# Longer contiguous pieces per partition in the weight loads of a one-token decode block

## The chip, the cores and the metric

The kernel runs on one core of a Trainium2 chip. The metric is the device time of one execution in microseconds (us): the median of three runs of the kernel before is 101.41 us, and the three lie between 101.40 and 101.51 us. A profile of one further execution was taken; it ran 101.79 us, of which 100.5 us lie between its first and its last instruction (the span). The other 1.3 us are start and end of the launch.

## The reference

One token (a row `x` of 1024 numbers) goes through an attention block with a key and value cache and through a two-layer perceptron; both read the same normalised row and both results are added to `x`. Everything is bf16.

```python
xn = _layernorm(x)                                   # 1 x 1024
# attention over the last W = 4096 cached positions, 32 query heads on 4 key/value heads
q = (xn @ wq)                                        # 1024 x 4096: 32 heads of 128
k = repeat(k_cache[:, :, Sk - W:, :], 8); v = repeat(v_cache[:, :, Sk - W:, :], 8)
p = softmax(q . k * 128 ** -0.5)
a = (p . v).reshape(1, 4096) @ wo                    # 4096 x 1024
# perceptron on a second layer norm
h = gelu(_layernorm(xn) @ w1 + b1)                   # 1024 x 3584
m = h @ w2 + b2                                      # 3584 x 1024
out = x + a + m
```

With a single row there is hardly any arithmetic per byte. The weights and the cache that are read come to 39.86 MB: wq 8.4 MB, w1 7.3 MB, keys 4.2 MB, values 4.2 MB, w2 7.3 MB, wo 8.4 MB.

## The kernel before, in words

**Layout of the weights.** Each weight matrix is spread over the 128 partitions so that one partition holds consecutive rows of the matrix: 8 rows of wq, 8 rows of w1, 28 rows of w2, 32 rows of wo. What one partition needs therefore lies in one contiguous piece of the memory. A list of numbers (`WQ_CHUNKS`, `W1_CHUNKS`, `W2_CHUNKS`, `WO_CHUNKS`, lines 22 to 25) says in how many loads a matrix comes and how many rows per partition each load brings. `load_rows` (line 142) issues one DMA per number. A chunk of 2 rows of wq is a piece of 16 KB for each of the 128 partitions; a chunk of 2 rows of w1 is 14 KB; 9 rows of w2 are 18 KB; 8 rows of wo are 16 KB. Each load has a semaphore of its own, and the matrix engine waits for it before the first matmul that reads the chunk.

**The order of the loads.** All big loads are issued by SyncE (SP) on one queue: four of wq, four of w1, two of keys, two of values (line 204). SP then waits until the matmuls on w1 are done (`sp.wait_ge(PE.sem, C["h"])`, line 316), because w2 is put over w1 and wo is put over wq in the on-chip memory, and issues four of w2 and six of wo. The two biases and the row `x` come on ScalarE's queue (lines 152 to 154).

**The order of the matmuls.** TensorE (PE) runs one program in order: the layer norm's sums; the bias b1 as the start of the accumulators (line 271, after a wait for its load); wq chunk by chunk (line 279, 8 matmuls of 512 columns a row, 64 in all); w1 chunk by chunk (line 294, 7 matmuls a row, 56 in all); the transposes of the keys (line 370) and of h (line 335); the scores (line 396); the first chunk of w2 (line 437, 4 matmuls of 256 columns a row, each on its own quarter of the array's columns); the softmax's total (line 450); the values (line 460, 64 matmuls); the second chunk of w2; the transpose of the attention's result (line 477); the other chunks of w2; and wo chunk by chunk (line 437 again, 128 matmuls in all). All of w2 and wo adds up in one accumulator, which ScalarE copies out (line 492) and SP stores (line 494). VectorE (DVE) and ScalarE (ACT) do the softmax between the scores and the values (lines 402 to 424).

**Matmuls without a use.** After chunk `j` of wo, PE runs the matmuls that `KEEP_BUSY[j]` lists (line 488). They read data that is there already and write to a bank of the accumulator memory that nobody reads any more; the list has one entry for each chunk of wo, six after the second chunk and four after the third.

Of the kernel before, what the change touches and what calls it, by code (L numbers as in the profile page):

```python
# [18 lines left out]
FC = F // 128  # L19
KC = D // 128  # L20
NQ = HQ * DH
WQ_CHUNKS = [2, 2, 2, 2]
W1_CHUNKS = [2, 2, 2, 2]
W2_CHUNKS = [9, 9, 8, 2]
WO_CHUNKS = [8, 8, 8, 6, 1, 1]
KEEP_BUSY = [[], [512] * 6, [512] * 4, [], [], []]
NPAIR = HKV // 2
PB = 2 * NBLK
OUTSIDE = -1e30
# [15 lines left out]
def bass_parallel_sum__sliding_block_cached__mixer_channel_mlp__decode_kernel(  # L45
# [20 lines left out]
    def sems(name, n):  # L66
        return [nc.alloc_semaphore(f"{name}{i}") for i in range(n)]

    s_xrow, s_b1, s_b2, s_out = (nc.alloc_semaphore(n) for n in ("s_xrow", "s_b1", "s_b2", "s_out"))
    s_wq = sems("s_wq", len(WQ_CHUNKS))  # L70
    s_w1 = sems("s_w1", len(W1_CHUNKS))
    s_k = sems("s_k", NPAIR)
    s_v = sems("s_v", NPAIR)
    s_wo = sems("s_wo", len(WO_CHUNKS))
    s_w2 = sems("s_w2", len(W2_CHUNKS))

# [65 lines left out]
    def load_rows(dst, src, chunks, width, semaphores):  # L142
        c0 = 0
        for j, n in enumerate(chunks):
            sp.dma_start(  # L145
                dst[:, c0 * width:(c0 + n) * width].rearrange("p (c n) -> p c n", c=n),
                src[:, c0:c0 + n, :],
            ).then_inc(semaphores[j], 16)
            c0 += n
# [49 lines left out]

    load_rows(WA, wq_p, WQ_CHUNKS, NQ, s_wq)  # L200
    load_rows(W1, w1_p, W1_CHUNKS, F, s_w1)
    for dst, cache, semaphores in ((KT, A_k_cache, s_k), (V, A_v_cache, s_v)):
# [71 lines left out]
    k = 0  # L274
    for j, n in enumerate(WQ_CHUNKS):
        pe.wait_ge(s_wq[j], 16)
# [12 lines left out]
    k = 0  # L289
    for j, n in enumerate(W1_CHUNKS):  # L290
        pe.wait_ge(s_w1[j], 16)
# [24 lines left out]
    sp.wait_ge(PE.sem, C["h"])  # L316
    load_rows(W2, w2_p, W2_CHUNKS, D, s_w2)
    load_rows(WA, wo_p, WO_CHUNKS, D, s_wo)

# [112 lines left out]
    def out_rows_mms(weights, vec, chunks, semaphores, j, stop_at=None):  # L432
        c0 = sum(chunks[:j])
        pe.wait_ge(semaphores[j], 16)
        for c in range(c0, c0 + chunks[j]):
            for a in range(4):
                ins = pe.matmul(acc(a), lhsT=vec[:, c:c + 32],  # L437
                                rhs=weights[:, c * D + a * 256: c * D + (a + 1) * 256],
                                start=False, stop=(c == stop_at))
        return ins  # L440
# [6 lines left out]
    pe.wait_ge(DVE.sem, C["d_GT"])  # L447
    out_rows_mms(W2, GT, W2_CHUNKS, s_w2, 0)
    pe.wait_ge(DVE.sem, C["sump"])
# [21 lines left out]
    with nc.allow_low_precision(reason="one of the two terms is not zero"):  # L471
        C["on"] = DVE.mark(dve.tensor_reduce(
            out=ON[:, :], in_=ONM[:, :].rearrange("p (g d) -> p d g", g=NPAIR), axis=AX.X, op=ALU.add))
    out_rows_mms(W2, GT, W2_CHUNKS, s_w2, 1)
    pe.wait_ge(DVE.sem, C["on"])
# [5 lines left out]
    C["OT"] = DVE.mark(dve.tensor_copy(OT[:, 0:32], PS[:, 5 * 512:5 * 512 + 32]))  # L481
    for j in range(2, len(W2_CHUNKS)):
        out_rows_mms(W2, GT, W2_CHUNKS, s_w2, j)
    pe.wait_ge(DVE.sem, C["OT"])
    for j in range(len(WO_CHUNKS)):
        last = out_rows_mms(WA, OT, WO_CHUNKS, s_wo, j, stop_at=31)
        for n in KEEP_BUSY[j]:
            pe.matmul(PS[0:32, 0:n], lhsT=OT[:, 0:32], rhs=WA[:, 0:n])
# [37 lines left out]
```

## Time and profile before

| What | Value |
|---|---|
| median of three runs | 101.41 us |
| the profiled execution | 101.79 us |
| its span | 100.5 us |
| PE busy | 70.3 us of the span |
| DVE, ACT busy | 25.4 and 12.8 us |
| bytes read, mean rate | 39.86 MB, 397 GB/s |
| packets on SP's load queue | 3176 |
| granted clock of PE, mean | 0.881 |

How to read it: PE, DVE, ACT, POOL and SP are the engines; "PEld" is PE's loading of the stationary operand, which overlaps its matmuls. The DMA share is the mean busy share of the 16 DMA engines that one core has; a packet is one contiguous piece that one of them moves. The granted clock is the share of full speed that TensorE was given. A chain of waits is followed back from the last instruction: at each step to what released it. Times inside the profile are counted from the start of the span.

### The profile page before, as it was taken

Reading aid. Unit: us, or ns where it says so; the run is one execution under the profiler, and the core shown is the slowest. Engines: PE = TensorE matmul, PEld = TensorE weight load, DVE = VectorE, ACT = ScalarE, POOL = GpSimd, SP = SyncE. Lnnn points to the kernel's source line nnn. Section 1 sums busy time; section 2 is a strip of 40 time slices with the busy share of each in tenths; the row PEclk is TensorE's granted clock in tenths of the full one; section 3 lists DMA queues with packets and bytes.
Section 4 is the critical chain, followed back from the end, with each engine's and each line's share of the span. In section 5 each row is a group of like instructions: output and inputs, shape, how many; then the busy total and the mean of one; then the engine's idle time right before and its main releaser. Section 6 shows DMA issues by size and latency. Waiting matters only on the chain.

```text
span 100.5 us, 1676 instructions
## 1 busy us (share of the span) xinstructions
PE 70.3 (70%) x762; PEld 41.3 (41%) x762; DVE 25.4 (25%) x48; ACT 12.8 (13%) x15; POOL 5.6 (6%) x22
## 2 busy tenths in 40 slices
PE   1309999999995738664999891652099999081961
PEld 1204224344332212224999591250078887041440
DVE  0574000000100000035859608474900030000000
ACT  2203300000000000031717600015000000000001
POOL 6870000000000000000000000000000000000000
PEclk9999999999999999999999985555557999999655
DMA  3999999999999999999999999999999999999920
GB/s 99 385 440 430 417 424 417 443 441 416 428 422 423 428 422 436 424 430 443 424 450 417 417 452 403 418 462 395 425 398 463 417 424 430 417 430 412 391 83 1
DMA packets 3188, 39.96 MB, mean 397 GB/s; under 512 B 359, under 2 KB 363, under 8 KB 750
## 3 DMA queue, kind: packets, MB, share of 16 engines
q1 hardware_dynamic: 3176, 39.85, 93.9%
q8 instruction: 6, 0.10, 0.4%
q10 hardware_dynamic: 6, 0.01, 0.0%
HBM read 39.86 MB, written 0.00 MB: 396 GB/s over the span
## 4 chain that ended last, share of the span: by engine, by line
DMA 82%; SPq 9%; PE 5%; issue 1%; ACT 0%
DMA WA<-in_A_wo_dram 45%; DMA W<-in_B_w_dram 37%; SPq L145 9%; PE PS L294 3%; PE PS L437 2%; ACT ORow L492 0%; PE PS L303 0%
## 5 line engine op out<-in xcount | busy, mean ns | idle before, releaser
L279 PE MATMUL PS<-WA,XNZ 128*8 128x512 bf16 x64 | 15.9, 415 | 0.0
L294 PE MATMUL PS<-W,YTb 128*1 128x512 bf16 x56 | 12.7, 379 | 4.3 <-DMA W<-in_B_w_dram 4.3
L279 PEld LDWEIGHTS PS<-WA,XNZ 128*8 128x8 bf16 x64 | 5.9, 93 | 10.4 <-issue 3.5
L294 PEld LDWEIGHTS PS<-W,YTb 128*1 128x1 bf16 x56 | 4.4, 83 | 12.7 <-DMA W<-in_B_w_dram 5.8
L437 PE MATMUL PS<-WA,OT 128*32 128x256 bf16 x128 | 5.1, 309 | 6.1 <-DMA WA<-in_A_wo_dram 6.1
L370 PE MATMUL PS<-identb,KV 128*128 128x128 bf16 x128 | 7.5, 219 | 2.2 <-DVE ROW L309 2.2
L460 PE MATMUL PS<-KV,Pb 128*32 128x256 bf16 x64 | 8.8, 310 | 0.0
L370 PEld LDWEIGHTS PS<-identb,KV 128*128 128x128 bf16 x128 | 7.2, 98 | 2.3 <-ACT ROW L307 2.3
L460 PEld LDWEIGHTS PS<-KV,Pb 128*32 128x32 bf16 x64 | 7.0, 110 | 1.6
L437 PEld LDWEIGHTS PS<-WA,OT 128*32 128x32 bf16 x128 | 3.5, 107 | 8.1 <-DMA WA<-in_A_wo_dram 7.8
L377 DVE COPY KV<-PS 128x1024 bf16<-128x1024 bf16 x10 | 6.3, 683 | 1.5 <-PE PS L370 1.5
L309 DVE CAST ROW<-PS 1x2048 bf16<-1x2048 f32 x1 | 2.3, 2278 | 16.4 <-PE PS L294 16.4
L382 ACT ACTIVATE KV<-PS 128x1024 bf16<-128x1024 bf16 x6 | 5.8, 1018 | 2.8 <-PE PS L370 2.8
L307 ACT ACTIVATE ROW<-PS 1x1536 bf16<-1x1536 f32 x1 | 1.4, 1440 | 33.4 <-PE PS L294 33.4
L437 PE MATMUL PS<-W,GT 128*32 128x256 bf16 x112 | 4.9, 320 | 1.0 <-DMA W<-in_B_w_dram 1.0
L286 DVE CAST Q<-PS 8x512 bf16<-8x512 f32 x1 | 0.7, 679 | 17.4 <-PE PS L279 17.4
L437 PEld LDWEIGHTS PS<-W,GT 128*32 128x32 bf16 x112 | 3.5, 110 | 1.8 <-issue 1.5
L492 ACT ACTIVATE ORow<-PS 128x256 bf16<-128x256 f32 x1 | 0.4, 385 | 29.2 <-PE PS L437 29.2
L424 DVE TENSOR_REDUCE SUMP<-Pb 128x32 f32<-128x2048 bf16 x1 | 3.6, 3566 | 1.9 <-ACT Pb L422 1.9
L396 PEld LDWEIGHTS PS<-QT,KV 128*128 128x128 bf16 x128 | 3.3, 98 | 0.4 <-issue 0.4
L396 PE MATMUL PS<-QT,KV 128*128 128x16 bf16 x128 | 3.4, 171 | 0.0
L450 PE MATMUL PS<-onesf,SUMP 128*32 128x1 f32 x2 | 0.3, 202 | 4.4 <-DVE SUMP L424 4.4
(91 smaller groups left out, 44.8 us busy)
## 6 DMA issues: line engine op xcount, KB each, us to landing
WA<-in_A_wq_dram SPq DMA_DIRECT2D x4, 2048.0 KB, 14.0
W<-in_B_w_dram SPq DMA_DIRECT2D x4, 1792.0 KB, 30.6
WA<-in_A_wo_dram SPq DMA_DIRECT2D x3, 2048.0 KB, 41.1
W<-in_B_w_dram SPq DMA_DIRECT2D x2, 2304.0 KB, 24.5
KV<-in_A_k_cache_dram SPq DMA_DIRECT2D x2, 2048.0 KB, 43.2
KV<-in_A_v_cache_dram SPq DMA_DIRECT2D x2, 2048.0 KB, 47.4
W<-in_B_w_dram SPq DMA_DIRECT2D x1, 2048.0 KB, 31.5
WA<-in_A_wo_dram SPq DMA_DIRECT2D x1, 1536.0 KB, 45.6
```

The costliest lines, as they stand in the source:

```text
L145: sp.dma_start(dst[:, c0 * width:(c0 + n) * width].rearrange("p (c n) -> p c n", c=n), src[:, c0:c0 + n, :],).then_inc(semaphores[j], 16)
L279: last = pe.matmul(PS[0:8, 7 * 512:8 * 512], lhsT=XNZ[:, 15 * k + 7 - t:15 * k + 15 - t], rhs=WA[:, k * NQ + t * 512: k * NQ + (t + 1) * 512],
L294: last = pe.matmul(PS[0:1, t * 512:(t + 1) * 512], lhsT=YTb[:, k:k + 1], rhs=W1[:, k * F + t * 512: k * F + (t + 1) * 512], start=False, s ...
L307: C["a_hrow"] = ACT.mark(act.activation(out=Hrow[:, 0:1536], in_=PS[0:1, 0:1536], func=ACTF.Copy))
L309: C["d_hrow"] = DVE.mark(dve.tensor_copy(Hrow[:, 1536:F], PS[0:1, 1536:F]))
L370: last = pe.matmul(PSb[:, o:o + 128], lhsT=KT[:, col + bb * 128: col + (bb + 1) * 128], rhs=identb[:, :], is_transpose=True)
L377: C["dkt"][u] = DVE.mark(dve.tensor_copy(KT[:, col + 1024 * s: col + 1024 * (s + 1)], PSb[:, bk * 1024:(bk + 1) * 1024]))
L382: C["akt"][u] = ACT.mark(act.activation(out=KT[:, col + 1024: col + 2048], in_=PSb[:, bk * 1024:(bk + 1) * 1024], func=ACTF.Copy))
L396: last = pe.matmul(PS[:, o:o + 2 * REP], lhsT=KT[:, (i * PB + b) * 128:(i * PB + b + 1) * 128], rhs=QT[:, i * 2 * REP:(i + 1) * 2 * REP], ...
L424: C["sump"] = DVE.mark(dve.tensor_reduce(out=SUMP[:, :], in_=Pb[:, :].rearrange("p (b n) -> p n b", b=PB), axis=AX.X, op=ALU.add))
L437: ins = pe.matmul(acc(a), lhsT=vec[:, c:c + 32], rhs=weights[:, c * D + a * 256: c * D + (a + 1) * 256], start=False, stop=(c == stop_at))
L460: last = pe.matmul(PS[0:32, 4 * 512:4 * 512 + NPAIR * DH], lhsT=Pb[:, b * HQ:(b + 1) * HQ], rhs=V4[:, :, b, :], start=(b == 0), stop=(b == ...
```

## The change

The rows per partition are split into fewer and larger loads; the bytes, their order and the places in the on-chip memory stay as they are. A load of 4 rows of wq brings 32 KB to each partition, one of 4 rows of w1 28 KB, one of 18 rows of w2 36 KB, one of 16 rows of wo 32 KB. The later chunks of w1, w2 and wo keep their size. `KEEP_BUSY` follows the new list of chunks of wo: two matmuls after its first chunk (16 rows) where six stood after the second of 8 rows, four after the next chunk as before. PE's program takes the first 18 rows of w2 ahead of the softmax's total and the values, where it took 9 before; the 8 rows after the values and the last 2 rows follow.

```diff
-WQ_CHUNKS = [2, 2, 2, 2]
-W1_CHUNKS = [2, 2, 2, 2]
-W2_CHUNKS = [9, 9, 8, 2]
-WO_CHUNKS = [8, 8, 8, 6, 1, 1]
-KEEP_BUSY = [[], [512] * 6, [512] * 4, [], [], []]
+WQ_CHUNKS = [4, 4]
+W1_CHUNKS = [4, 2, 2]
+W2_CHUNKS = [18, 8, 2]
+WO_CHUNKS = [16, 8, 6, 1, 1]
+KEEP_BUSY = [[512] * 2, [512] * 4, [], [], []]
```

## The prediction

> **What bounds the kernel now.** I read the page's slices first, then the chain of waits, then the DMA answer for one quiet stretch, then PE's order of time, then the clock near the end. The page's DMA row:
>
> ```profile
> DMA  3999999999999999999999999999999999999920
> ```
>
> The DMA engines are over 90% busy in 37 of 40 slices, from 2.5 us to 95 us, while PE idles often. The chain of waits says the same; its last pieces (start, us, what):
>
> ```profile
> 41.06 3.18 PE PS L294 x14
> ...
> 44.44 0.17 SPq L145
> ...
> 50.79 45.64 DMA WA<-in_A_wo_dram
> ...
> 96.48 1.92 PE PS L437 x32
> 98.40 0.02 issue
> 98.43 0.39 ACT ORow L492
> ```
>
> The end is set by the load of 6 rows of wo, landed at 96.44 us, with 4.1 us of fixed work behind it. It is late because the whole stream of 39.86 MB is in front of it, not because SP issued it late: when w1's matmuls end (44.24 us) the keys and values are still arriving until 60.7 us (the trace's semaphore records, which I also use for other landings). So the question is what one byte in that stream costs. From 12 to 22 us there are only pieces of 16 KB:
>
> ```profile
> DMA packets 299, 4.28 MB, mean 428 GB/s; under 512 B 37, under 2 KB 37, under 8 KB 37
> ...
> q1 hardware_dynamic: 299, 4.28, 100.0%
> ```
>
> 262 packets of 16 KB and 37 tiny ones (a load's completion marks) fill 16 engines for 10 us: 160 us / 262 = 0.61 us each, back to back. The trace's record of each packet has the medians 84 ns for 2 KB, 159 for 4 KB, 465 for 12 KB, 535 for 14 KB, 611 for 16 KB, 691 for 18 KB and 9 ns for a mark. The line through 2 KB and 16 KB is 8.7 ns + 36.8 ns per 1000 bytes; it gives 159 for 4 KB and 536 for 14 KB. So a packet has a fixed part of about 8.7 ns.
>
> **Part 1: fewer packets on the stream.** Per engine (8 partitions each) the data packets are now wq 32, w1 32, keys and values 32, w2 32, wo 48 = 176, with 22 marks; 16 x 198 + 8 of the output = 3176, the page's count. After: 16 + 24 + 32 + 24 + 40 = 136 and 17 marks, 2456 on the page. Saved per engine: 40 x 8.7 + 5 x 9 = 393 ns, all of it before the load of 6 rows. Nothing covers it, since that load is waited for. Bounds: a packet of 28 to 36 KB is not in this trace (largest 18 KB). If such pieces are cut again, the gain is 0. If a bigger packet also saved 25 ns more each, as the spread of a few rows would allow (18 KB packets lie between 686 and 694, 12 KB between 460 and 468), it would be 1.4 us, a far end; the other far end is the next part's. I take 0.39, because the line holds over six sizes.
>
> The Trainium skill ("DMA: Bandwidth & Descriptors", section on the anatomy of one DMA, measured on GpSimd's path) has a fixed cost of about 2.0 us per DMA. By it five fewer DMAs would save up to 10 us and end at 91.4. The row speaks against it here: wq's four loads land 4.9 us apart, which is 8 x 0.61, so nothing fixed is left between them.
>
> **Part 2: what shares the stream.** Six packets of 16 KB on another queue (q8, "instruction") break in, at 30.9, 53.8, 61.4, 76.5, 87.0 and 95.8 us; each takes 1.0 to 1.1 us and the packet beside it takes 1.08 to 1.18 us in place of 0.61. Five engines are 1.05 us late at the end for this, and the 96.44 is theirs. I take the same 1.05: the added bytes are the same 16 KB. If the lateness grows with the packet beside it (twice as big at three or four of the fetches), it is up to 2.1 us: a loss of 1.05. The biases b1 and b2 wait likewise: b1's packet started at 5.6 us, about six packets of wq after it was asked for; six of 32 KB make that about 9.6, landed by about 11 us. Its matmuls (3.1 us) then end at about 14.3.
>
> **Part 3: later data for PE.** *wq*: 4 rows are there at 13.0 us (the second landing before), PE starts at 14.3 in place of 11.29; 32 matmuls at 0.25 us (15.88 / 64) end by 22.3, the other 4 rows land at 22.7 and end at 30.7. *w1*: 4 rows land at 31.3, 28 matmuls at 0.227 (3.18 / 14) end at 37.6, 14 more at 40.8; the last two rows land at about 40.8 and end at 44.0. Before it was 44.24, so SP's wait and the keys' transposes behind it do not move by over 0.3 us. Were this cover gone, SP would still have 16 us before the queue runs dry. *w2*: this is the real move.
>
> ```profile
> 66.36 2.11 PE L437 MATMUL PS<-W,GT 128*32 128x256 bf16 x36 [1.02 <-DMA W<-in_B_w_dram]
> 72.91 0.27 PE L450 MATMUL PS<-onesf,SUMP 128*32 128x1 f32 x2 [4.44 <-DVE SUMP L424]
> 73.12 8.62 PE L460 MATMUL PS<-KV,Pb 128*32 128x256 bf16 x62
> ...
> 84.27 1.05 PE L437 MATMUL PS<-WA,OT 128*32 128x256 bf16 x32
> 87.72 1.06 PE L437 MATMUL PS<-WA,OT 128*32 128x256 bf16 x32 [2.41 <-DMA WA<-in_A_wo_dram]
> 88.61 1.46 PE L488 MATMUL PS<-WA,OT 128*32 128x512 bf16 x6
> 92.74 1.06 PE L437 MATMUL PS<-WA,OT 128*32 128x256 bf16 x32 [2.67 <-DMA WA<-in_A_wo_dram]
> 93.63 1.85 PE L488 MATMUL PS<-WA,OT 128*32 128x512 bf16 x4
> 96.48 1.90 PE L437 MATMUL PS<-WA,OT 128*32 128x256 bf16 x32 [1.00 <-DMA WA<-in_A_wo_dram]
> ```
>
> Here PE works on 9 rows of w2 at 66.4 us, idles 4.4 us for the softmax's sum, and runs the values. After, it waits for 18 rows, which land when the second 9 did, 71.7 - 0.3 = 71.4. 72 matmuls at the half clock (2.11 / 36) take 4.2 us, to 75.6; the total and the values stand behind them, 2.7 us later than before, at 75.9. The values took 3.5 us at half clock (to 76.6) and 5.1 at full: 0.215 and 0.108 us each. With the clock rising at 76.6 again, 3 slow and 61 fast end at 83.2, the other ten rows of w2 (1.05 + 0.27) and the attention's transposes between them end near 84.9. wo's first 16 rows land at 87.7 - 0.4 = 87.3, so the cover is 2.4 us. 64 matmuls (2.1) and two idle ones (0.4) end at 89.9; 8 rows land at 92.3, end with four idle ones at or before 95.2; the 6 rows land at 96.05. Cost: 0.
>
> **Part 4: the clock at the end.**
>
> ```profile
> 90.60:91.30 0.70, 0.00 (x0) 0.00 (x0) 0.00 (x0) 0.00 (x0) 0.00 (x0) 1.00 0.99 421
> ...
> 93.40:94.10 0.70, 0.70 (x18) 0.42 (x10) 0.00 (x0) 0.00 (x0) 0.00 (x0) 0.70 1.05 442
> ...
> 96.90:97.60 0.70, 0.70 (x20) 0.54 (x16) 0.00 (x0) 0.00 (x0) 0.00 (x0) 0.50 0.06 21
> ```
>
> (The third number from the end is the clock.) It falls to a half at about 93.7, and the last 32 matmuls take 1.92 us where 32 took 1.06. After, PE is busy about 12.3 us between 76.6 and 93.7 where it was 12.0, with idle stretches of 2.4 us where they were 2.4 and 2.7. I take the same fall: 0. Were the clock full, the end would be 97.65 - 0.39 (the last row's landing) + 0.2 = 97.46 in place of 98.40 - 0.39: 0.55 better. Were it full in the timed runs before and half after: 0.55 worse.
>
> The Trainium skill ("TensorE: Matmul & The Clock Gate", section on HAM oscillation) warns of idle stretches over about 3.4 us, which larger chunks lengthen. Here the clock fell after one of only 2.7 us, so the trace does not bear out that limit; by the page the 2.4 us stretches would leave it full and end at 100.5.
>
> **Sum.** -0.39 + 0 + 0 + 0: the span 100.5 becomes 100.1 and the profiled execution 101.79 becomes 101.4; the median lies 0.38 below the profiled one, so 101.41 - 0.39 = **101.0 us**.
>
> **The rivals.**
> *A, forecast, 101.0 (0.48).* Own range 100.8 to 101.2.
> *B, the packets are cut again, or the 8.7 ns are spent otherwise: 101.4 (0.18).* For it: no packet above 18 KB was seen. Against: 14, 16 and 18 KB pieces are all one packet.
> *C, the same and a full clock at the end: 100.45 (0.11).* For it: a little more PE work in the deciding stretch. Against: it fell with nearly the same.
> *D, slower: a fetch of instructions beside packets of 32 to 36 KB holds its engine longer.* The lateness must grow by over 0.39 us to decide; at the full 1.05 it is 102.1 (0.18). For it: the neighbour packet is stretched by about its own length. Against: the fetch's bytes are the same.
> *E, slower: the clock stays at a half through the values.* 64 x 0.215 = 13.8, from 75.9 to 89.7; then wo's work runs behind its loads at half speed and ends about 4.3 us later: 105.7 (0.05). It decides only if the clock rises after about 86 us, 10 us of unbroken work; before, it rose 3.5 us after work began.
>
> **How the numbers follow.** A difference of 0.2% (0.2 us) is about what a measurement can tell. Faster: A and C, 0.59; within: B, 0.18; slower: D and E, 0.23. The range leaves out E and the outer part of C and D: 100.4 to 102.0, about 0.85.
>
> **What would show it.** Part 1: 2456 packets on q1, each 32 KB packet at about 1.21 us, the 6 rows landing near 96.05. Part 2: late engines by 1.05 us as before; b1 landed by 11 us. Part 3: values start near 75.9, PE waits at wo's first chunk. Part 4: half clock and 1.9 us in the last group. I would be wrong if 32 KB take over 1.22 us, if the late engines are later, or if PE never waits for wo.

## The result and the profile after

The changed kernel takes 101.22 us (median of 17 runs, 101.06 to 101.31), the kernel before on the same chip 101.46 us (median of 17, 101.30 to 101.94): 0.9971 of it, 95% interval 0.9962 to 0.9981. It is faster by 0.29% (0.29 us by the ratio, 0.24 by the medians). The forecast was 101.0 us, 0.39 us faster; the range was 100.4 to 102.0. Ratios here and below are taken over the fast runs, those within 1.5% of the fastest run of their kernel; only the last two kernels below have others. The profiled execution took 101.22 us with a span of 99.9 us, against 101.79 and 100.5 before. That difference, 0.57 us, is twice the one of the medians, and the sections below show why.

The load queue on the page of the changed kernel (packets, MB, share of 16 engines):

```profile
q1 hardware_dynamic: 2456, 39.85, 94.1%
```

720 packets fewer than before, as counted. The DMA answer for 12 to 22 us, where now only pieces of 32 KB arrive:

```profile
DMA packets 161, 4.42 MB, mean 442 GB/s; under 512 B 25, under 2 KB 25, under 8 KB 25
```

442 GB/s stand where 428 stood (a stretch of 10 us holds few big packets, so its ends weigh). The trace's packet records have medians of 1062 ns for 28 KB, 1213 ns for 32 KB and 1364 ns for 36 KB. The line laid through 2 KB and 16 KB of the kernel before gives 1063, 1213 and 1364. So the big pieces are single packets, and the record of each holds the same fixed 8.7 ns as that of a small one.

The end of the chain of waits of the changed kernel (start, us, what):

```profile
40.99 3.18 PE PS L294 x14
...
47.69 49.69 DMA WA<-in_A_wo_dram
97.38 0.04 issue
97.42 0.32 PE PS L437 x4
97.74 0.02 issue
97.77 0.38 ACT ORow L492
```

It is still the load stream that ends last, but another load of it. Before, the last 32 matmuls ran on from the landing of the 6 rows, 1.92 us at half clock, and hid the landings of the two single rows. Now PE is done with the 6 rows and the first single row in time and waits for the last single row (97.38 us). PE's order of time around w2 and wo (start, us, line, count, and the wait before):

```profile
71.57 3.63 PE L437 MATMUL PS<-W,GT 128*32 128x256 bf16 x72 [4.66 <-DMA W<-in_B_w_dram]
75.02 0.20 PE L450 MATMUL PS<-onesf,SUMP 128*32 128x1 f32 x2
75.08 6.93 PE L460 MATMUL PS<-KV,Pb 128*32 128x256 bf16 x62
...
83.43 0.40 PE L437 MATMUL PS<-W,GT 128*32 128x256 bf16 x8
87.80 3.17 PE L437 MATMUL PS<-WA,OT 128*32 128x256 bf16 x64 [3.96 <-DMA WA<-in_A_wo_dram]
90.71 1.06 PE L488 MATMUL PS<-WA,OT 128*32 128x512 bf16 x2
92.46 1.06 PE L437 MATMUL PS<-WA,OT 128*32 128x256 bf16 x32 [0.69 <-DMA WA<-in_A_wo_dram]
93.34 1.03 PE L488 MATMUL PS<-WA,OT 128*32 128x512 bf16 x4
96.15 0.95 PE L437 MATMUL PS<-WA,OT 128*32 128x256 bf16 x28 [1.78 <-DMA WA<-in_A_wo_dram]
97.42 0.29 PE L437 MATMUL PS<-WA,OT 128*32 128x256 bf16 x4 [0.33 <-DMA WA<-in_A_wo_dram]
```

The values start 2 us later than before (75.08 for 73.12) and nothing comes of it: PE idles 3.96 us before wo's first load. PE takes up the 6 rows at 96.15, 0.33 us earlier than before. And the clock stretches at the end (the clock is the third number from the end):

```profile
89.00:92.00 3.00, 2.77 (x41) 1.69 (x30) 0.00 (x0) 0.00 (x0) 0.00 (x0) 0.55 0.97 411
...
96.50:97.00 0.50, 0.50 (x24) 0.31 (x12) 0.00 (x0) 0.00 (x0) 0.00 (x0) 1.00 0.14 53
```

In this execution the half clock fell on wo's first 16 rows, where there was time, and the last group ran at full clock. So the two profiles differ in two things: 0.3 us of stream, and the clock of the last group.

### The profile page after: what moved, and what is told of

It reads as the page before. It is cut to its first block, busy times and chain, and to the rows that moved or that the text cites. A ratio compares the mean times of both kernels' runs of the same rounds, so it can differ in the third digit from the quotient of the medians.

```text
span 99.9 us, 1663 instructions
## 1 busy us (share of the span) xinstructions
PE 69.5 (70%) x758; PEld 42.8 (43%) x758; DVE 25.4 (25%) x48; ACT 12.9 (13%) x15; POOL 5.6 (6%) x22
## 3 DMA queue, kind: packets, MB, share of 16 engines
q1 hardware_dynamic: 2456, 39.85, 94.1%
## 4 chain that ended last, share of the span: by engine, by line
DMA 88%; SPq 5%; PE 4%; issue 1%; ACT 0%
DMA WA<-in_A_wo_dram 50%; DMA W<-in_B_w_dram 38%; SPq L145 5%; PE PS L294 3%; ACT ORow L492 0%; PE PS L437 0%; PE PS L303 0%
## 5 line engine op out<-in xcount | busy, mean ns | idle before, releaser
L370 PE MATMUL PS<-identb,KV 128*128 128x128 bf16 x128 | 9.1, 242 | 2.2 <-DVE ROW L309 2.2
L370 PEld LDWEIGHTS PS<-identb,KV 128*128 128x128 bf16 x128 | 8.8, 110 | 2.3 <-ACT ROW L307 2.3
L437 PE MATMUL PS<-W,GT 128*32 128x256 bf16 x112 | 5.4, 348 | 4.7 <-DMA W<-in_B_w_dram 4.7
L437 PEld LDWEIGHTS PS<-WA,OT 128*32 128x32 bf16 x128 | 4.1, 112 | 8.9 <-DMA WA<-in_A_wo_dram 4.4
L460 PE MATMUL PS<-KV,Pb 128*32 128x256 bf16 x64 | 7.1, 272 | 0.0
L437 PEld LDWEIGHTS PS<-W,GT 128*32 128x32 bf16 x112 | 4.0, 123 | 5.7 <-issue 5.1
L460 PEld LDWEIGHTS PS<-KV,Pb 128*32 128x32 bf16 x64 | 6.1, 97 | 0.8
L402 DVE TENSOR_REDUCE MXP<-PS 128x32 f32<-128x2048 f32 x1 | 2.3, 2292 | 3.9 <-PE PS L396 3.9
```

What stands on the lines that cost most here:

```text
L370: last = pe.matmul(PSb[:, o:o + 128], lhsT=KT[:, col + bb * 128: col + (bb + 1) * 128], rhs=identb[:, :], is_transpose=True)
L402: C["mxp"] = DVE.mark(dve.tensor_reduce(out=MXP[:, :], in_=PS[:, 0:2048].rearrange("p (b n) -> p n b", b=PB), axis=AX.X, op=ALU.max))
L437: ins = pe.matmul(acc(a), lhsT=vec[:, c:c + 32], rhs=weights[:, c * D + a * 256: c * D + (a + 1) * 256], start=False, stop=(c == stop_at))
L460: last = pe.matmul(PS[0:32, 4 * 512:4 * 512 + NPAIR * DH], lhsT=Pb[:, b * HQ:(b + 1) * HQ], rhs=V4[:, :, b, :], start=(b == 0), stop=(b == ...
```

## The experiments

Three theories stood against each other. *Packets*: every packet costs about 8.7 ns on the stream that sets the end. *Loads*: the cost is per load, so five fewer loads are the gain. *Order*: the gain comes from PE's program, the matmuls without a use and the clock at the end. Twelve kernels were run, in groups that share a chip and the runs of the kernel before.

**The same loads in short pieces.** The loads keep their number, size and place, but each takes every second row (w2's first load two rows of three), so that a partition's share comes in pieces of one or two rows:

```diff
-            src[:, c0:c0 + n, :],
+            src[:, rows[0]:rows[-1] + 1:step, :],   # wq: rows 0,2,4,6, then 1,3,5,7; likewise the others
```

> The changed kernel with the same 13 weight loads, in the same sizes and at the same places of PE's program, but each load takes every second row of its matrix (in w2's first load two rows of three), so that one partition's share comes in pieces of one or two rows in place of one long piece. Per engine 136 + 424 = 560 data packets in place of 136, and 17 marks as before. Theory 'packets' (8.7 ns per packet on the stream that sets the end): 424 x 0.0087 = 3.7 us slower than the changed kernel, 104.9 us. Rival 'loads' (the gain comes from five fewer loads, 0.29 / 5 = 0.06 us each): no change against the changed kernel, 101.2. Rival 'order' (the gain comes from PE's order, the matmuls without a use and the clock at the end): 101.2 too.

Measured: 105.43 us, 1.0381 of the kernel before (1.036 to 1.0402). Its load queue and the end of its chain of waits:

```profile
q1 hardware_dynamic: 9240, 39.85, 95.6%
```

```profile
91.16 10.50 DMA WA<-in_A_wo_dram
101.66 0.04 issue
101.70 0.32 PE PS L441 x4
```

With nothing changed but the length of the pieces (and with it which rows come first) the last row lands at 101.66 us in place of 97.38, and the end follows it. *Loads* and *order*, which both said 101.2, cannot account for this: pieces have a price. Of the 4.28 us, 0.43 are a later first packet (2.26 us for 1.82); 3.85 are left for 424 packets per engine, 9.1 ns each, for pieces of 2 to 8 KB. That the same thing made the changed kernel faster is for the halves and the pairs below.

**One row per load.** PE's order as in the changed kernel, with its matmuls without a use at the same places, 76 weight loads:

```diff
-WQ_CHUNKS = [4, 4]
-W1_CHUNKS = [4, 2, 2]
-W2_CHUNKS = [18, 8, 2]
-WO_CHUNKS = [16, 8, 6, 1, 1]
+WQ_CHUNKS = [1] * 8
+W1_CHUNKS = [1] * 8
+W2_CHUNKS = [1] * 28
+WO_CHUNKS = [1] * 32
```

> The changed kernel with one row per load: 76 weight loads in place of 13, PE's order as in the changed kernel. Per engine 640 data packets in place of 136 and 80 marks in place of 17. Theory 'packets': 504 x 0.0087 + 63 x 0.009 = 4.95 us slower than the changed kernel, 106.2. Rival 'loads' at 0.06 us each: 63 x 0.06 = 3.8 us slower, 105.0, and well above the kernel with the same pieces in 13 loads. Rival 'order': 101.2.

Measured: 105.56 us, 1.0404 (1.0375 to 1.0433), with 11,528 packets on the queue and the last row at 101.67 us. It has 63 more loads and 80 more data packets per engine than the kernel above and lands its last row at the same time, with a first packet that starts 0.42 us earlier: all of them together cost 0.43 us on the stream. Five fewer loads at that price are 0.03 us at most, so a load has no price of its own that would make the gain. The time was 4.3 us above the changed kernel where 4.95 were expected. The Trainium skill ("DMA: Bandwidth & Descriptors", section on the anatomy of one DMA) has 2.0 us fixed per DMA, measured on GpSimd's path for one DMA; by it, as an estimate, 63 more loads in a row would be 126 us. On this queue, where the next load always stands behind, the runs show none of it.

**Each half alone.** First wq and w1, then w2 and wo with their list of matmuls:

```diff
 # the early half, against the kernel before
-WQ_CHUNKS = [2, 2, 2, 2]
-W1_CHUNKS = [2, 2, 2, 2]
+WQ_CHUNKS = [4, 4]
+W1_CHUNKS = [4, 2, 2]
```

```diff
 # the late half, against the kernel before
-W2_CHUNKS = [9, 9, 8, 2]
-WO_CHUNKS = [8, 8, 8, 6, 1, 1]
-KEEP_BUSY = [[], [512] * 6, [512] * 4, [], [], []]
+W2_CHUNKS = [18, 8, 2]
+WO_CHUNKS = [16, 8, 6, 1, 1]
+KEEP_BUSY = [[512] * 2, [512] * 4, [], [], []]
```

> Only wq in 4+4 and w1 in 4+2+2; w2, wo and the matmuls without a use as in the kernel before. Per engine 24 data packets and 3 marks fewer than before. Theory 'packets': 0.24 us faster than before, 101.22. Rival 'loads': three of the five, 0.17 faster, 101.29. Rival 'order': no change, 101.46, since PE's program behind the scores is the old one.

> Only w2 in 18+8+2 and wo in 16+8+6+1+1 with their list of matmuls without a use; wq and w1 as in the kernel before. Per engine 16 data packets and 2 marks fewer than before. Theory 'packets': 0.16 us faster than before, 101.30. Rival 'loads': 0.12 faster, 101.34. Rival 'order': the whole gain, 101.17.

Measured: early half 101.43 us, 0.9989 (0.9974 to 1.0004); late half 101.33, 0.9983 (0.9971 to 0.9995). The two add up to the whole change (0.11 + 0.17 = 0.28%), but these times don't say how the gain is shared: each interval holds the values of all three theories. The traces say more. Averaged over the 16 engines, the last row lands at 96.54 to 96.58 us in three profiles with the old loads, at 96.44 with the early half, 96.45 with the late half, and at 96.22 to 96.43 (mean 96.30) in four with all the new loads. So each half brings the stream forward by 0.11 to 0.12 us, and both by 0.26. PE's order can't do that: the only wait of SP's loads on PE ends at about 44.4 us in both kernels, while keys and values still arrive until 60.5 us or later. The very last landing is that of the slowest engine and varies more (97.52 for the early half and 97.69 for the late one, against 97.67 on average with the old loads).

**The changed kernel again,** as the neighbour of the next three:

> The changed kernel itself, as the neighbour for the others of this group: 0.29% under the kernel before, within its interval (0.9962 to 0.9981).

Measured: 101.24 us, 0.9971 (0.9957 to 0.9986).

**The clock at the end, in the changed kernel.** More matmuls without a use, and none:

```diff
-KEEP_BUSY = [[512] * 2, [512] * 4, [], [], []]
+KEEP_BUSY = [[512] * 6, [512] * 10, [], [], []]
+    for _ in range(12):        # after w2's last chunk
+        pe.matmul(PS[0:32, 0:512], lhsT=GT[:, 0:32], rhs=W2[:, 0:512])
```

> The changed kernel with more matmuls without a use, so that TensorE hardly idles after the values: 12 of 512 columns after w2's last chunk, 6 in place of 2 after wo's first chunk, 10 in place of 4 after its second. Same loads. Theory 'packets', with a clock at the end that differs from run to run: the end is then always the landing of the last single row (97.4 in the changed kernel's profile) and 0.32 us of PE behind it; 101.1 us, and runs that lie closer together than the 0.25 us of the changed kernel. Rival 'the clock at the end has no share in the times': as the changed kernel, 101.2, with the same spread. Against both: if the clock is still low in the first gap, 12 matmuls at half clock (5.1 us) pass the landing of wo's first chunk and the end is up to 1 us later.

```diff
-KEEP_BUSY = [[512] * 2, [512] * 4, [], [], []]
+KEEP_BUSY = [[], [], [], [], []]
```

> The changed kernel without any matmuls without a use. Same loads. Theory 'packets' with the clock: the clock is a half in the last group in most runs, 28 matmuls take up to 1.7 us from 96.15 in place of 0.95 and the end is about 0.3 us later than the changed kernel's: 101.5. Rival 'the clock at the end has no share': 101.2.

Measured: with more 101.26 us, 0.9962 (0.9949 to 0.9975), 101.17 to 101.39; with none 101.51 us, 0.9992 (0.9979 to 1.0004). More of them bring no measurable gain over the changed kernel (0.9971), only a smaller spread than its neighbour's 101.11 to 101.68. Leaving all of them out costs 0.27 us by the medians (101.51 for 101.24) and 0.21 by the ratios, about as expected: the end of that chain of waits is the old one, the landing of the 6 rows and 1.93 us of PE:

```profile
96.13 1.93 PE PS L437 x32
98.05 0.02 issue
98.07 0.38 ACT ORow L492
```

**The clock at the end, in the kernel before.** The same pair on the old loads:

```diff
-KEEP_BUSY = [[], [512] * 6, [512] * 4, [], [], []]
+KEEP_BUSY = [[512] * 8, [512] * 14, [512] * 10, [], [], []]     # more
+KEEP_BUSY = [[], [], [], [], [], []]                            # none
```

> The kernel before, with more matmuls without a use: 8, 14 and 10 of 512 columns after wo's first, second and third load, so that TensorE's clock stays up to the end. Loads as before. If the kernel before lost time to a half clock in its last group: with 97.66 us as the landing of its last row and 0.32 us of PE behind it, 98.0 in place of 98.40 in its profile; up to 0.4 us faster in the runs that had it, and 101.3 as a median if half of them did. Theory 'packets': it stays 0.3 us above the changed kernel with the same cure (101.26 there), that is 101.55, the time of the kernel before, if few of its runs had the half clock. Rival 'order': it comes down to the changed kernel's 101.25, and the loads have no share.

> The kernel before without any matmuls without a use. Loads as before. Against the changed kernel without them (0.9992 of the kernel before) only the loads and the order of w2 differ, and the clock at the end is a half in both. Theory 'packets': 0.3 to 0.4 us above that one, 101.85. Rival 'order': the same as that one, 101.5.

Measured: with more 101.64 us, 0.9994 (0.9981 to 1.0007); with none 101.86 us, 1.002 (1.0005 to 1.0034), the runs within 0.17 us of each other. With more, up to 0.4 us of gain in the runs with a half clock was expected, and the ratio shows none. In its profile the clock rose only at 81.0 us, the values ran until 84.9, and PE was busy with matmuls without a use past the landing of the 6 rows at 96.40, so that the end of the chain of waits is PE and no landing:

```profile
94.92 1.73 PE PS L488 x8
...
96.99 1.05 PE PS L437 x25
98.04 0.02 issue
98.06 0.39 ACT ORow L492
```

In this execution, the fastest of the twelve, that costs next to nothing: the last row landed at 97.67 us, and 4 matmuls behind it (0.32 us) would have ended at the same time. The others took up to 0.48 us longer; whether for this reason is not shown. The end of the chain of waits of the kernel with none:

```profile
96.47 1.93 PE PS L437 x27
98.39 0.02 issue
98.42 0.38 ACT ORow L492
```

The two kernels with none of them settle the matter. At half clock in both profiles, old loads end at 1.002 and new ones at 0.9992: 0.28%, and the intervals (1.0005 to 1.0034 and 0.9979 to 1.0004) do not overlap. The gain is there without any help of the clock, and the last group waits for the same load, 0.34 us earlier in these two profiles (96.13 for 96.47; over the three old and four new profiles that load's landings differ by 0.25). The pair with more of them says 0.32% (0.9994 and 0.9962), but there the old loads may have paid for their extra matmuls. The clock in the last group is worth another 0.2 to 0.26 us: the kernel before without them is 0.20 slower by the ratio and 0.26 by the medians (101.86 against 101.60). The profiled execution of the kernel before, 101.79 us with a half clock in its last group, was one that paid it; 14 of the 17 runs behind the result lie between 101.30 and 101.54 and, by their times, seem not to have paid. That is the other half of the 0.57 us between the two profiles.

**Still fewer packets.** Three candidates for a faster kernel:

```diff
 # first, against the changed kernel
-W2_CHUNKS = [18, 8, 2]
-WO_CHUNKS = [16, 8, 6, 1, 1]
+W2_CHUNKS = [18, 10]
+WO_CHUNKS = [16, 8, 6, 2]
 # second: W1 [4, 4], W2 [18, 10], WO [24, 6, 1, 1], 20 + 4 matmuls without a use
 # third: W1 [4, 2, 2], W2 [18, 10], WO [24, 6, 1, 1], 24 + 3 matmuls without a use
```

> The changed kernel with two loads merged further: w2 in 18+10, wo in 16+8+6+2. Per engine 16 data packets and 2 marks fewer. Theory 'packets': 0.16 us faster on the stream, of which the last group gives back 0.1 (8 matmuls behind the last landing in place of 4): 101.15. Rival 'loads': 0.12 faster less the same 0.1: 101.2. It tells the two apart by too little; it is run as a candidate for a faster kernel.

> A candidate for a faster kernel: w1 in 4+4, w2 in 18+10, wo in 24+6+1+1, 20 matmuls without a use after w2's last load and 4 after wo's first. Per engine 24 data packets and 3 marks fewer than in the changed kernel. Theory 'packets': 0.24 us under the changed kernel, 101.0, if PE still reaches wo before its loads: w1 ends 3.2 us later (47.4), the values end near 85 us, wo's 24 rows land near 92.3 and end near 95, the 6 rows land near 95.9. Against: if PE is late, it is slower than the changed kernel.

> The last candidate with w1 back in 4+2+2, so that PE is not 3 us late for the values: w2 in 18+10, wo in 24+6+1+1, 24 matmuls without a use after w2's last load and 3 after wo's first. Per engine 16 data packets and 2 marks fewer than in the changed kernel. Theory 'packets': 0.16 us under the changed kernel, 101.1 (0.9955 of the kernel before), with its runs close together, since PE reaches wo's 24 rows by about 89.5 us and they land near 92.3. If the spread of the last candidate came from the clock in the last 5 us and not from PE being late for the values, the spread of 2 us is here too.

Measured (medians of all runs): 101.32 us, 0.9975 (0.9962 to 0.9988); 101.65 us, 0.9985 (0.9961 to 1.001), from 100.99 to 103.23; 101.84 us, 1.0001 (0.9977 to 1.0025), from 100.98 to 102.97. None beats the changed kernel. The stream did get shorter: the last row lands at 97.28, 97.30 and 97.31 us. The first gives it back in its last group (8 matmuls behind the landing in place of 4): they took 0.61 us in place of 0.29, as the clock fell to a half at 97.38 us in this execution, just ahead of them. The other two reach the forecast 101.0 in their best runs; 13 of their 24 runs lose 0.5 to 1.1 us against those, and five lose about 2, of which none was profiled. In the profile of the second (102.11 us) PE is late: the values start at 79.3 us, at half clock until 83.5, and the matmuls without a use run on past the landing of the 24 rows of wo at 92.36:

```profile
79.32 8.96 PE L460 MATMUL PS<-KV,Pb 128*32 128x256 bf16 x62
...
89.71 4.06 PE L485 MATMUL PS<-W,GT 128*32 128x512 bf16 x18
...
93.83 2.99 PE L437 MATMUL PS<-WA,OT 128*32 128x256 bf16 x90
```

In the third PE is in time. Its order of time, and its clock:

```profile
83.85 5.35 PE L485 MATMUL PS<-W,GT 128*32 128x512 bf16 x24
92.49 4.39 PE L437 MATMUL PS<-WA,OT 128*32 128x256 bf16 x96 [3.29 <-DMA WA<-in_A_wo_dram]
96.70 0.38 PE L490 MATMUL PS<-WA,OT 128*32 128x512 bf16 x1
```

```profile
89.00:92.00 3.00, 0.20 (x1) 0.00 (x0) 0.00 (x0) 0.00 (x0) 0.00 (x0) 1.00 0.72 307
92.00:95.00 3.00, 2.51 (x49) 2.20 (x52) 0.00 (x0) 0.00 (x0) 0.00 (x0) 0.56 0.97 397
```

After 3.3 us of waiting the clock falls just as the 96 matmuls begin. They take 4.39 us where 96 at full clock would take 2.8 (at full clock 32 took 1.06 us in the changed kernel and 64 took 1.93 in the one with no matmuls without a use, so 32 more are 0.87), pass the landing of the 6 rows, and the three matmuls meant to hold the clock stand in front of the last group. PE ends at 98.42, 1.1 us after the last landing. So this execution (101.94 us) loses its time not by PE being late for the values, as the second did, but by the clock in the last 6 us. That the whole spread of either comes from these two is not shown.

## Why the prediction was right, and where a size was off

- **What bounds it: right.** Averaged over the engines, the last row landed earlier in every kernel with fewer packets and later in both with more, and the end followed unless PE was late. The one engine that ends last adds up to 0.2 us of its own: with the late half it was no earlier than before (97.69 us).
- **Part 1, right in kind, too large in size.** The count (2456), the time of a 32 KB packet (1213 ns for "about 1.21") and the line for three new sizes hold exactly. The term was put at 0.39 us. The ratio gives 0.29 (0.19 to 0.38); the landing of the 6 rows is 0.25 earlier (96.42 on average in the three profiles with the old loads, 96.17 in the four with the new ones; 0.33 to 0.34 in the two profiles shown), that of the last row 0.22 (97.67 and 97.45), and the mean over the engines 0.26. The mean over the engines also shows where the rest is lost, over the same seven profiles. Each merge of two big loads should bring 0.079 us (8 packets and a mark). The first load of wq lands 0.006 us earlier, the second adds 0.086, w1's first adds 0.016 by the end of w1, and the two in w2 and wo together add 0.15. So three of five merges bring what the term says, and the first of wq and that of w1 bring almost nothing. (In the late half, which leaves wq and w1 as they were, the mean landings at the same places differ from the old ones by up to 0.04 us, so this is coarse.) For wq it fits that its first packets take 1.47 to 1.98 us for 32 KB where the later ones take 1.21; no run isolated that, and for w1 the cause stays open. Added packets and marks don't cost one price throughout either: 9.1 ns each in the first kernel with short pieces, and 80 and 63 more of them in the second cost 0.43 us where the terms give 1.26. The forecast's far ends (cut packets: nothing; 25 ns more each: 1.4 us) are both excluded.
- **Part 2, right on the fetches, wrong on b1.** The fetches of instructions took 0.98 to 1.11 us beside the bigger packets, and the late engines are late by 1.1 us as before; rival D did not come about. But b1 did not wait for six packets: its packet started at 6.15 us, not 9.6, and its matmuls began at 8.06. Before, with packets half as big, it started at 5.6; with wq in pieces of 8 KB at 3.7 and 4.8. What it waits for stays open. PE so took up wq at 13.06 us and not at 14.3. The step cost nothing, since PE waits for wq until then anyway.
- **Part 3, right.** w1 ended at 44.17 us (forecast 44.0), the 18 rows of w2 were taken up at 71.57 (71.4), the values started at 75.08 (75.9), wo's three waits ended at 87.80, 92.46 and 96.15 (87.3, 92.3, 96.05). The cover ahead of wo was 3.96 us, not 2.4, as the clock rose earlier, at 74.7 us.
- **Part 4, the weak step.** "I take the same fall" was read from one execution. The clock's phase differs from run to run: the changed kernel's profile ended at full clock. How many of the timed runs did isn't shown, but the ratio (0.29%) and the two kernels at half clock (0.28%) agree, so the term was near 0, by luck as far as the reason given goes. The sum started from an execution that had paid 0.2 to 0.26 us for it, and came right by taking off the 0.38 us to the median; C's condition in the profile did not bring C's 0.55: with a full clock the end is at the landing of the last row plus 0.36 us (97.74), and the profile gained 0.57 in all, not 0.94.
- **Rival E** did not come about in the changed kernel. A version of it did in the profile of the second candidate: half clock into the values and wo's work behind its loads, though at full clock again by then. (E's 105.7 counts its 4.3 us from the time before; counted from the forecast, as the other rivals are, it would be 105.3.)

## What to carry to other kernels

Where a profile shows DMA engines busy from end to end, take the packet records, lay a line through duration against size, and multiply its fixed part by the packets per engine that an edit removes. Here that came out at 0.39 us where 0.22 to 0.29 were measured: an upper bound, and a fair one. Number of loads is not the price, number of pieces is; but each merged load delays the work behind it, and once that work can run into the last landing, as in the profiles of the last two candidates, further merging loses more than it saves. A single profiled execution can sit at one end of the spread: look whether something in it, here the clock of the last group, differs from run to run before starting a sum from it.

## What the runs showed that was not expected

- The clock changes in steps of one length: in the changed kernel it held for 30.7, 3.4, 10.2, 13.7, 13.7, 3.4 and 6.8 us, all whole multiples of 3.41. The Trainium skill ("TensorE: Matmul & The Clock Gate", section on the HAM clock gate) gives such a window of about 3.4 us that runs free of the kernel's start, and the runs agree: the same kernel's steps began at 16.6 us in one profile and at 17.2 in the next.
- It fell for one such step at 47.3 us in the changed kernel, 0.8 us after the end of a wait of only 2.24 us: the first 48 transposes of the keys then took 4.47 us in place of 2.84. Here it was hidden.
- A DMA engine that meets a fetch of instructions (16 KB, every 8 to 23 us) stays late by about 1.1 us to the end, as if each engine had a fixed share of every load. In the profiles of both kernels five of 16 engines are late so, and the end is theirs.
- SP's issue set no limit even with 60 loads after w1 and 11,528 packets: the last row landed at the same time as with short pieces in 13 loads (101.67 and 101.66 us).
